# Gated linear attention, routed experts and a gated layer in one kernel: the last attention unit, the first pass's transposes and the last routing step change places

## The chip, the cores and the metric

The kernel runs on one core of a Trainium2 chip, as one launch. Time is device time in microseconds (us), and lower is better. The kernel before has a median of 864.84 us over three runs (859.22, 864.84 and 869.75 us). A core has five engines that run side by side and meet at semaphores: PE (matrix products; its weight loads are shown apart as PEld), DVE (vector), ACT (activation), POOL (general purpose, and here the issuer of indirect DMAs) and SP (issuer of the other DMAs). Each runs its own instructions strictly in the order written.

## The reference: what is computed

Three stages follow one another. `q`, `k`, `v` and `f_logit` are [4, 8, 768, 48]; there are 3072 tokens of 384 numbers.

```python
f = 1.0 / (1.0 + np.exp(-f_logit))
for t in range(S):                                   # attention: a decayed running state per head
    state = f[:, :, t, :, None] * state + np.einsum('bhd,bhe->bhde', k[:, :, t], v[:, :, t])
    y[:, :, t] = np.einsum('bhd,bhde->bhe', q[:, :, t], state)
...
logits = x @ w_gate                                  # experts: each token goes to one of 8
e_idx = np.argmax(logits, axis=1)
gate_w = probs[np.arange(N), e_idx]                  # probs: softmax of the logits
eom = 1.0 / (1.0 + np.exp(-(x @ w_output_gate)))
for e in range(E):
    h = np.maximum(x[mask] @ w1[e], 0.0)
    out[mask] = gate_w[mask, None] * eom[mask, e, None] * (h @ w2[e])
...
gate = 1.0 / (1.0 + np.exp(-(x @ w_gate)))           # gated layer, 384 -> 1536 -> 384
out = (gate * (x @ w_val)) @ w_out
```

## The kernel before, in words

**Attention** is cut into 24 units of 128 tokens (four sequences of six units). A loop `for i in range(1, NU)` writes the order by hand. In round i the kernel scores unit i (`s_score`, tile `pS`), makes keys `kT` and queries `qT` of unit i+1, masks the scores (`s_mask`, tile `am`), scans the logarithms of unit i+2 (`s_sum`, tile `ls`), forms the output of unit i-1 (`s_y`: products into `pY`, which ACT copies to `xT`), advances the state (`s_state`, tiles `pM`, `sn`), transposes the keys of the next unit (`s_turn`, tile `pk`), transposes `xT` back to rows (`s_rows`, tile `px`, copied by ACT to `x`) and takes 16 logits from `xT` (`s_logit`, tile `plg`, copied by DVE to `lg`).

**Routing** runs over groups of units: 0 to 5, 6 to 11, 12 to 16, 17 to 21 and 22 to 23. `route(u0, n)` is a generator of three parts: the arg max on DVE (`m` to `oh`), the selected gate (`ohf`, `sel`), and then the rank of each token in its expert (small products into `pr` on PE, then some thirteen short DVE operations up to the factor `meta` and the count `carry`). `pr`, `plg` and the throw-away products of `keep_warm` share one bank of PSUM, so each waits until DVE has read the one ahead of it. `put_rows` then scatters the rows of routed units to HBM by indirect DMAs from POOL, after a small POOL copy that writes factor and number behind each row.

**Experts** run as nine passes. The first (p = 0) takes the first 192 rows of expert 0, which the routing of units 0 to 16 has filled. Its rows are gathered at the start of round 23, scaled by their factors on DVE (`scale`), transposed on PE (`to_xt`, tile `ptx`), and cast by ACT and DVE to a high and a low part (`xt`). A pass has 8 steps f; each makes 9 products into `ph` (`proj`), then `hh` on ACT and `hl` on DVE, and two steps later 9 products into `po` (`down`). The second pass takes the rest of expert 0 (304 rows), the others the experts 1 to 7 in the order of a plan that is made on the chip from the counts (`make_plan`, with one product into `pf` that sums the counts). The loads of the next expert's weights and the gather of the third pass's rows go by the plan, since the expert's number stands in their addresses; the gather of the second pass's rows waits for the last scatter alone. After the passes comes the gated layer, six groups of 512 tokens.

**The stretch that the change touches** lies between round 17 and the start of the second pass. Before, the order there is: rounds up to 23, `scale`, `s_y(23)`, `to_xt(0)`, two DMAs of token numbers (`put_ids`), the rest of the routing of units 17 to 21, five scatters; then the first pass, with `s_rows(23)` and `s_logit(23)` behind its step 0, the first part of the last routing behind step 1, and the rest of it, two scatters, the gather of the second pass and the plan behind step 2. The output `xT` of unit 23 and the rows of units 19 to 23 lie in slots of the weight ring, which outlive the attention's memory; the other rows lie in a pool of the attention stage.

Of the kernel before, what the change touches and what calls it, by code (L numbers as in the profile page):

```python
# [8 lines left out]
F32 = mybir.dt.float32  # L9
# [11 lines left out]
P = 128  # L21
# [7 lines left out]
def kernel(  # L29
# [17 lines left out]
    nc = tc.nc  # L47
# [6 lines left out]
    HP = H // 2  # L54
# [3 lines left out]
    NU = B * NCH  # L58
# [11 lines left out]

    SOON = 12

    LATE = 19

    W0 = 192

# [2 lines left out]
    PD = P // 2 + D  # L79
# [3 lines left out]


    NWARM = 22
    WARM = (2, 2, 3)

    const = ctx.enter_context(tc.tile_pool(name="const", bufs=1))
    drp = ctx.enter_context(tc.tile_pool(name="drp", bufs=1, space=DRAM))
# [138 lines left out]
    def kill(key):  # L228
        dead.setdefault(key, len(dead))

    ring_s = Slots(ring, "ring", NRING)
# [141 lines left out]
    puts = []  # L373

    def put_rows(most):
        for u in puts[0:most]:
            nc.gpsimd.tensor_copy(xrow[u][:, DM:XW].bitcast(I32), meta[:, u, :].bitcast(I32))
            put = nc.gpsimd.indirect_dma_start(
                out=xs_all[:, :],
                out_offset=bass.IndirectOffsetOnAxis(ap=sidx[:, u : u + 1], axis=0),  # L380
                in_=xrow[u],
                in_offset=None,
                bounds_check=NSL - 1,
                oob_is_err=False,
            )

            tc.declare_no_dep(put.ins, group="rows", reason="distinct rows")
            tc.add_to_no_dep_group("rows", put.ins)
            del xrow[u]
            if u >= LATE:  # L390
                kill(("x", u))
            if u >= EARLY:
                tc.add_to_no_dep_group("late rows", put.ins)
            else:
                early_puts.append(put.ins)
        del puts[0:most]

    xts = {}
    xg = {}
# [93 lines left out]
    def s_logit(u):  # L493
        d = st.pop(u)
        pl = bank_po(MISC, [P, 2 * NE], "plg")
        for hp in range(HP):
            nc.tensor.matmul(pl, lhsT=d["xT"][:, hp, :], rhs=wgp[:, hp, :], start=(hp == 0), stop=(hp == HP - 1))  # L497
        nc.vector.tensor_copy(lg[:, u % (NU // 2), :], pl)
        if u >= LAST:
            kill(("xT", u))  # L500

    with ExitStack() as actx:
        ap1 = actx.enter_context(tc.tile_pool(name="ap1", bufs=1))
# [125 lines left out]
        def s_y(u):  # L629

            c = u % NCH
            d = st[u]
            pY = bank_po(1 + u % 2, [P, HP, P], "pY")
            so = sbd.get(u)
            vt = tin["v", u].rearrange("p h d -> p (h d)")

            for hp in range(HP):
                for j in range(2):
                    at = half(j, True)
                    h0 = (2 * hp + j) * D  # L640
                    nc.tensor.matmul(  # L641
                        pY[at, hp, :], lhsT=vt[:, h0 : h0 + at.stop - at.start], rhs=d["am"][:, j, hp, :],
                        start=(hp == 0), stop=(c == 0), skip_group_check=True,
                    )
            if c:
                for hp in range(HP):
                    for j in range(2):
                        at = half(j)
                        nc.tensor.matmul(  # L649
                            pY[at, hp, :], lhsT=so[at, hp, :], rhs=d["qT"][at, hp, :], start=False, stop=True,  # L650
                            skip_group_check=True,
                        )
            if u < LAST:
                xT = wk.tile([PD, HP, P], F32, name="xT")
            else:
                xT = ring_s.tile(("xT", u), [P, HP * P], F32, "xTlate").rearrange("p (h t) -> p h t", h=HP)[0:PD]
            nc.scalar.copy(xT, pY[0:PD])
            d["xT"] = xT

        with tc.manual_schedule():  # L660
# [52 lines left out]
            def step_route():  # L713
                if routing and next(routing[0], True):
                    routing.pop(0)

            def on(fn, u, *a):
                if 0 <= u < NU:
                    fn(u, *a)

            for i in range(1, NU):
                if i == NU - 1:
                    gather_rows(0)
                s_score(i)
                if i == 1:
                    s_log(i + 2)
                    s_mask(i, 0)
                on(s_keys, i + 1)
                on(s_queries, i + 1)
                load("qk", i + 4)  # L730
                on(s_end, i)
                put_rows(2 if i < 19 else 3 if i < 22 else 6)
                if i > 1:
                    on(s_log, i + 2)
                    s_mask(i, 0)
                load("f", i + 6)
                s_mask(i, 1)
                on(s_sum, i + 2)
                step_route()
                s_y(i - 1)  # L740
                load("v", i + 4)
                s_state(i)
                on(s_turn, i + 1)
                s_rows(i - 1)
                s_logit(i - 1)
                for u0, n in groups:
                    if i - 1 == u0 + n - 1:
                        routing.append(route(u0, n))
                if i > 16:
                    step_route()  # L750
                if i == 1:
                    nc.gpsimd.memset(zrow, 0.0)
                if 2 <= i < 6:

                    for e in (2 * i - 4, 2 * i - 3):
                        nc.sync.dma_start(
                            xs_all[e * SLOT + LEAST : (e + 1) * SLOT, :].rearrange("(b p) d -> p b d", p=P),
                            zrow[:, :, 0:XW].to_broadcast([P, NB - LEAST // P, XW]),
                        )
                if i == 6:  # L760
                    feed.issue()
                if i >= 8:
                    feed.step(1)
            while feed.left():
                feed.step()
            scale(xg[0], passes[0][2], nc.vector)
            s_y(NU - 1)
            to_xt(0, xg[0], passes[0][2])
            for part in range(2):
                put_ids(0, part)  # L770
            for todo in routing:
                for _ in todo:
                    pass
            put_rows(6)

    with ExitStack() as mctx:
        NGW, NGO = 17, 11
# [236 lines left out]
        with tc.manual_schedule():  # L1014
# [24 lines left out]
            for i in range(len(units) + LAG):  # L1039
# [13 lines left out]
                    )  # L1053
                    hs[i] = (hh, hl)
                if i == 0:
                    s_rows(NU - 1)
                    s_logit(NU - 1)
                if i == 1:
                    routing = route(*groups[-1])
                    next(routing)  # L1060
                if i - LAG in hs:
                    down(i - LAG)
                if i < len(units):
                    p, f = units[i]
                    if planning:
                        for _ in range(2):
                            next(planning, None)
                    elif i == 2:
                        for _ in routing:
                            pass  # L1070
                        put_rows(6)
                        gather_rows(1)
                        planning = make_plan()
                        next(planning)
                    if f == PUT_AT and p:
                        put_pass(p - 1)
                    if f == 0 and p:
                        turn(p + 1)
                    if p > 1 or p and f >= 2:
                        feed.step(3, ring_s.free)  # L1080
                    if p >= 2:
                        conv.step(1)
                    elif p:
                        conv.issue()
                    if len(who) == NE and not feed.left():
                        split_glu(1)
                    if i == 20:
                        check()
                    if f == 2 and ids_left is not None:
                        put_ids(ids_left, 1)  # L1090
                        ids_left = None
                    if f == (7 if p == 0 else 3 if p == 1 else 1) and p + 1 < len(passes):
                        scale(xg[p + 1], passes[p + 1][2], None if p else nc.vector)
                    if p == 0 and f == 7:

                        down(i - 1)
                        down(i)
                        keep_warm(WARM[2])
                    if f == (4 if p else 7) and p + 1 < len(passes):
                        to_xt(p + 1, xg[p + 1], passes[p + 1][2])  # L1100
                        put_ids(p + 1, 0)
                        ids_left = p + 1
                        if p:
                            gather_rows(p + 2)
                    if p == len(passes) - 1:
                        if f == 1:
                            gather_tok(0)
                        if f == 5:
                            tok_parts(0)
# [265 lines left out]
```

## Time and profile before

| | |
|---|---|
| median of three runs | 864.84 us (859.22 to 869.75) |
| the profiled execution | 866.66 us, span in the trace 865.0 us |
| PE busy | 843.2 us, 97% of the span |
| DVE, ACT, POOL busy | 463.4, 351.5, 211.2 us |
| granted PE clock, mean | 0.983 of full |
| attention, first pass, end of the last expert pass (us of the span) | 0 to 142, 142 to 172, to 403 |

The span runs from the first to the last instruction. In the rows below, a timeline row says: start, duration, engine, line, operation, output<-inputs, shapes and how many instructions were merged; in brackets the idle time of the engine ahead of it, and what ended that. Products are pipelined, so the step from one start to the next is what a product costs, not its duration. The granted clock is 1.00 at 2.4 GHz and 0.50 at 1.2 GHz.

### The profile page before, as it was taken

The numbers are of one execution on the slowest core, as the hardware profiler recorded it, in microseconds if no ns is written. First come the engines' busy times: TensorE is split into PE (matmuls) and PEld (weight loads), VectorE is DVE, ScalarE is ACT, GpSimd is POOL, SyncE is SP. The second block draws the span as 40 slices with busy tenths as digits, with TensorE's granted clock in tenths as the row PEclk, the third lists the DMA queues.
The fourth block names the chain that finished last, engine by engine and source line by source line (L and its number), as shares of the span: only waits on it lengthen the run. The fifth ranks groups of instructions, "written<-read, shape, count | busy, mean of one in ns | idle before, by whom it ended". The sixth has DMA issues, their size and how long they took to land.

```text
span 865.0 us, 14074 instructions
## 1 busy us (share of the span) xinstructions
PE 843.2 (97%) x5388; PEld 750.7 (87%) x5388; DVE 463.4 (54%) x866; ACT 351.5 (41%) x690; POOL 211.2 (24%) x201
## 2 busy tenths in 40 slices
PE   8999988999999999999999999999999999999995
PEld 5898878998899999998888888888888888888884
DVE  6888994468899998996543223221322322132221
ACT  7778772166556655654333212211221221122111
POOL 4227482104344554553200100100010010001001
PEclk9999998799999999999999999999999999999998
DMA  8999641656567677733100200010020000001001
GB/s 186 281 277 274 177 138 62 212 162 193 186 198 228 204 220 219 235 98 118 36 1 1 74 1 0 19 56 1 1 74 0 1 19 20 1 0 37 1 1 40
DMA packets 51582, 87.57 MB, mean 101 GB/s; under 512 B 12810, under 2 KB 32690, under 8 KB 51506
## 3 DMA queue, kind: packets, MB, share of 16 engines
q1 hardware_dynamic: 44882, 62.97, 25.1%
q0 software_dynamic: 6624, 23.62, 8.5%
q8 instruction: 44, 0.72, 0.3%
q14 instruction: 32, 0.26, 0.1%
HBM read 68.35 MB, written 18.22 MB: 100 GB/s over the span
## 4 chain that ended last, share of the span: by engine, by line
issue 50%; PE 37%; DVE 4%; POOL 3%; DMA 3%; ACT 2%; SPq 0%; POOLq 0%; DVEq 0%; ACTq 0%
PE ph L787 4%; PE ph L788 4%; PE ph L789 4%; PE po L788 4%; PE po L787 4%; PE po L789 4%; POOL out_dram L1000 2%; PE pS L588 2%; PE pY L641 2%; PE plg L497 2%; PE pY L649 2%; DMA st<-in_moe_w_dram 2%; DMA ft<-in_ft_dram 1%; PE ptx L423 1%; PE px L486 1%
## 5 line engine op out<-in xcount | busy, mean ns | idle before, releaser
L1131 DVE TENSOR_TENSOR hf<-pv,sg 128x512 f32<-128x512 f32 x72 | 49.8, 692 | 267.9 <-PE pv L789 264.1
L1000 POOL DMA_INDIRECT out_dram<-ob,ids x24 | 23.5, 980 | 404.2 <-DVE ob L999 398.7
L1127 ACT ACTIVATE sg<-pg 128x512 f32<-128x512 f32 x72 | 43.0, 598 | 173.9 <-PE pg L789 173.8
L1134 ACT CAST hh<-hf 128x512 fp32r<-128x512 f32 x72 | 44.7, 621 | 158.8 <-DVE hf L1131 158.8
L238 DVE TENSOR_TENSOR w_lo<-st,w_hi 128x384 fp32r<-128x384 f32 (+1 forms) x112 | 94.6, 875 | 9.5 <-ACT w_hi L237 8.5
L788 PE MATMUL po<-w_lo,hh 128*128 128x384 f32 x288 | 96.6, 335 | 0.0
L787 PE MATMUL po<-w_hi,hh 128*128 128x384 f32 x288 | 96.4, 335 | 0.0
L789 PE MATMUL po<-w_hi,hl 128*128 128x384 f32 x288 | 96.3, 334 | 0.0
L789 PE MATMUL pg<-xt_hi,w_lo 128*128 128x512 f32 x216 | 85.5, 396 | 0.0
L788 PE MATMUL pv<-xt_lo,w_hi 128*128 128x512 f32 x216 | 85.5, 396 | 0.0
L787 PE MATMUL pg<-xt_hi,w_hi 128*128 128x512 f32 x216 | 85.5, 396 | 0.0
L787 PE MATMUL pv<-xt_hi,w_hi 128*128 128x512 f32 x216 | 85.1, 394 | 0.0
L788 PE MATMUL pg<-xt_lo,w_hi 128*128 128x512 f32 x216 | 85.1, 394 | 0.0
L789 PE MATMUL pv<-xt_hi,w_lo 128*128 128x512 f32 x216 | 85.1, 394 | 0.0
L788 PE MATMUL po<-hl,w_hi 128*128 128x192 f32 (+8 forms) x216 | 75.7, 350 | 2.1 <-DVE hl L1051 2.1
L1135 DVE TENSOR_TENSOR hl<-hf,hh 128x512 fp32r<-128x512 f32 x72 | 49.9, 693 | 49.4 <-ACT hh L1134 49.4
L787 PE MATMUL po<-hh,w_hi 128*128 128x192 f32 (+8 forms) x216 | 75.7, 350 | 0.0
L789 PE MATMUL po<-hh,w_lo 128*128 128x192 f32 (+8 forms) x216 | 75.5, 350 | 0.0
L187 POOL TENSOR_SCALAR cva<-cva 128x512 f32<-128x512 f32 (+1 forms) x30 | 60.9, 2029 | 47.1 <-ACT cva L186 47.1
L1050 ACT ACTIVATE hh<-ph 128x192 fp32r<-128x192 f32 (+8 forms) x72 | 35.6, 494 | 85.9 <-PE ph L789 85.9
L787 PE MATMUL ph<-xt_hi,w_hi 128*128 128x304 f32 (+7 forms) x192 | 68.0, 354 | 0.9 <-DVE hl L1051 0.5
L237 ACT CAST w_hi<-st 128x384 fp32r<-128x384 f32 (+1 forms) x112 | 59.2, 558 | 20.1 <-PE po L788 20.0
(179 smaller groups left out, 1729.7 us busy)
## 6 DMA issues: line engine op xcount, KB each, us to landing
st<-in_moe_w_dram SPq DMA_DIRECT2D x48, 256.0 KB, 3.2
st<-in_moe_w_dram SPq DMA_DIRECT2D x32, 384.0 KB, 3.7
qk<-in_qkt_dram SPq DMA_DIRECT2D x48, 192.0 KB, 5.5
ft<-in_ft_dram SPq DMA_DIRECT2D x48, 96.0 KB, 5.5
v<-in_v_dram SPq DMA_DIRECT2D x24, 192.0 KB, 4.8
stg<-in_moe_w_gate_dram POOLq DMA_DIRECT2D x9, 512.0 KB, 4.0
stg<-in_moe_w_val_dram POOLq DMA_DIRECT2D x9, 512.0 KB, 3.9
stg<-in_moe_w_out_dram POOLq DMA_DIRECT2D x12, 384.0 KB, 3.4
```

The lines of the kernel that those rows point to most:

```text
L187: nc.gpsimd.tensor_scalar(out=af, in0=af, scalar1=HW_LEAST, scalar2=HW_MOST, op0=ALU.max, op1=ALU.min)
L237: nc.scalar.copy(hi, src)
L238: nc.vector.tensor_tensor(out=lo, in0=src, in1=hi.bitcast(F32), op=ALU.subtract)
L787: nc.tensor.matmul(ps, lhsT=ah, rhs=bh, start=first, stop=False)
L788: nc.tensor.matmul(ps, lhsT=ah, rhs=bl, start=False, stop=False)
L789: nc.tensor.matmul(ps, lhsT=al, rhs=bh, start=False, stop=last)
L1000: put = nc.gpsimd.indirect_dma_start(out=out[:, :], out_offset=bass.IndirectOffsetOnAxis(ap=idx[g][:, i : i + 1], axis=0), in_=ob, in_offs ...
L1050: nc.scalar.activation(out=hh, in_=pS, func=AF.Relu)
L1127: nc.scalar.activation(out=sg, in_=pg, func=AF.Sigmoid)
L1131: nc.vector.tensor_tensor(out=hf, in0=pv, in1=sg, op=ALU.mult)
L1134: nc.scalar.copy(hh, hf)
L1135: nc.vector.tensor_tensor(out=hl, in0=hf, in1=hh.bitcast(F32), op=ALU.subtract)
```

## The change

The last unit's output is computed in round 23, straight behind that of unit 22, and its `xT` lies in the attention's memory like the others. `scale` of the first pass's rows comes ahead of it. `to_xt(0)` follows the loop directly, then the rest of the routing of units 17 to 21 and its five scatters, and then `s_rows(23)`, `s_logit(23)`, the token numbers and the first part of the last routing. Its second part is issued behind step 0 of the first pass, its rest, the scatters, the gather and the plan behind step 1. In rounds 17 to 22 the extra routing step stands ahead of `s_rows` and of the line that appends a new group, so that a new group's first part runs one round later, behind that round's masks and scan. `put_rows` issues its copies first and then its scatters. Unit 18's rows move to the ring (`LATE`). At the end of the first pass one of three throw-away products goes, and the last `down` stands behind the transposes of the second pass.

```diff
-    LATE = 19
+    LATE = 18
...
-    WARM = (2, 2, 3)
+    WARM = (2, 2, 2)
...
         for u in puts[0:most]:
             nc.gpsimd.tensor_copy(xrow[u][:, DM:XW].bitcast(I32), meta[:, u, :].bitcast(I32))
+        for u in puts[0:most]:
             put = nc.gpsimd.indirect_dma_start(
...
-            if u < LAST:
-                xT = wk.tile([PD, HP, P], F32, name="xT")
-            else:
-                xT = ring_s.tile(("xT", u), [P, HP * P], F32, "xTlate").rearrange("p (h t) -> p h t", h=HP)[0:PD]
+            xT = wk.tile([PD, HP, P], F32, name="xT")
...
                 on(s_turn, i + 1)
+                if i == LAST:
+                    scale(xg[0], passes[0][2], nc.vector)
+                    s_y(i)
+                if i > 16:
+                    step_route()
                 s_rows(i - 1)
                 s_logit(i - 1)
                 for u0, n in groups:
                     if i - 1 == u0 + n - 1:
                         routing.append(route(u0, n))
-                if i > 16:
-                    step_route()
...
-            scale(xg[0], passes[0][2], nc.vector)
-            s_y(NU - 1)
             to_xt(0, xg[0], passes[0][2])
-            for part in range(2):
-                put_ids(0, part)
             for todo in routing:
                 for _ in todo:
                     pass
             put_rows(6)
+            s_rows(LAST)
+            s_logit(LAST)
+            for part in range(2):
+                put_ids(0, part)
+            routing = route(*groups[-1])
+            next(routing)
...
                 if i == 0:
-                    s_rows(NU - 1)
-                    s_logit(NU - 1)
-                if i == 1:
-                    routing = route(*groups[-1])
                     next(routing)
...
-                    elif i == 2:
+                    elif i == 1:
                         for _ in routing:
                             pass
                         put_rows(6)
...
                         down(i - 1)
-                        down(i)
                         keep_warm(WARM[2])
                     if f == (4 if p else 7) and p + 1 < len(passes):
                         to_xt(p + 1, xg[p + 1], passes[p + 1][2])
+                        if not p:
+                            down(i)
```

The rows below are the engines' instructions in the order written; the line numbers behind the change are one or a few off those of before.

First place: DVE in rounds 17 and 18, before. `lg` is the copy of unit 16's logits, with which the group 12 to 16 is complete.

```order
L498 COPY lg<-plg 128x16
L161 TENSOR_REDUCE m<-lg 128x5
L162 TENSOR_TENSOR t_1800<-lg,m 128x40
L163 TENSOR_TENSOR sc<-lg,m 128x40
L164 TENSOR_TENSOR sc<-sc,e_75 128x40
L165 TENSOR_REDUCE ms_all<-sc 128x5
L166 TENSOR_TENSOR oh<-sc,ms_all 128x40
L238 TENSOR_TENSOR w_lo<-st_1150,w_hi 128x512
L555 TENSOR_TENSOR kT<-qk_115,gi 112x512
L595 TENSOR_TENSOR am<-pS,tri 128x512 x2
L544 SCALAR_TENSOR_TENSOR ls<-runs_109,ln 112x512
```

The same place in the changed kernel:

```order
L499 COPY lg<-plg 128x16
L238 TENSOR_TENSOR w_lo<-st_1150,w_hi 128x512
L554 TENSOR_TENSOR kT<-qk_115,gi 112x512
L594 TENSOR_TENSOR am<-pS,tri 128x512 x2
L543 SCALAR_TENSOR_TENSOR ls<-runs_109,ln 112x512
L161 TENSOR_REDUCE m<-lg 128x5
L162 TENSOR_TENSOR t_1840<-lg,m 128x40
L163 TENSOR_TENSOR sc<-lg,m 128x40
```

The arg max of the group now stands behind the keys, the masks and the scan of the round, where it stood ahead of them.

Second place: PE behind the output of unit 23, before, and then behind the first products of the first pass, before.

```order
L641 MATMUL pY<-am,v 48x128
L649 MATMUL pY<-qT,sn 48x128 x8
L423 MATMUL ptx<-ident,xs 128x128 x3
L423 MATMUL ptx<-ident,xs 128x64 x3
L787 MATMUL ph<-xt_2381,w_hi 128x192
L788 MATMUL ph<-xt_2381,w_hi 128x192
```

```order
L788 MATMUL ph<-xt_2381,w_hi 128x192
L789 MATMUL ph<-xt_2381,w_lo 128x192
L486 MATMUL px<-ident,xTlate 128x112 x4
L497 MATMUL plg<-wgp,xTlate 128x16 x4
L787 MATMUL ph<-xt_2381,w_hi 128x192
```

The same two places in the changed kernel:

```order
L640 MATMUL pY<-am,v 48x128
L648 MATMUL pY<-qT,sn 48x128 x8
L487 MATMUL px<-ident,xT 128x112 x4
L498 MATMUL plg<-wgp,xT 128x16 x4
L424 MATMUL ptx<-ident,xs 128x128 x3
L424 MATMUL ptx<-ident,xs 128x64 x3
L330 LDWEIGHTS tris
L330 MATMUL pr<-oh,tris 128x40
```

```order
L336 LDWEIGHTS oneb
L336 MATMUL pr<-carry,oneb 128x40
L487 MATMUL px<-ident,xT 128x112 x4
L788 MATMUL ph<-xt_2354,w_hi 128x192
L789 MATMUL ph<-xt_2354,w_hi 128x192
L790 MATMUL ph<-xt_2354,w_lo 128x192
L498 MATMUL plg<-wgp,xT 128x16 x4
L788 MATMUL ph<-xt_2354,w_hi 128x192
```

The rows and logits of unit 22 now stand behind the output of unit 23; the routing products and unit 23's rows stand between the transposes `ptx` and the first `ph`, and unit 23's logits behind the first three of nine `ph`.

Third place: PE around the plan's product `pf`, before, and in the changed kernel.

```order
L788 MATMUL po<-hl,w_hi 128x192
L789 MATMUL po<-hh,w_lo 128x192
L884 MATMUL pf<-chk,onec 1x10
L787 MATMUL ph<-xt_2381,w_hi 128x192
L788 MATMUL ph<-xt_2381,w_hi 128x192
```

```order
L789 MATMUL po<-hl,w_hi 128x192
L790 MATMUL po<-hh,w_lo 128x192
L885 MATMUL pf<-chk,onec 1x10
L788 MATMUL ph<-xt_2354,w_hi 128x192
L789 MATMUL ph<-xt_2354,w_hi 128x192
```

Before, `pf` stands behind 36 `ph` and 18 `po` of the first pass; now behind 27 `ph` and 9 `po`.

## Rows read from the trace of the kernel before

**Rows 1.** The page: busy time, share and instructions of PE.

```profile
PE   843.2 (97%) x5388; PEld 750.7 (87%) x5388; DVE 463.4 (54%) x866; ACT 351.5 (41%) x690; POOL 211.2 (24%) x201
```

**Rows 2.** Busy time by stretch: length, engines' busy time, granted clock, DMA.

```profile
140.00:142.00 2.00, 1.08 (x12) 0.63 (x8) 1.33 (x7) 0.59 (x1) 0.78 (x2) 1.00 0.00 0
142.00:143.00 1.00, 0.68 (x4) 0.42 (x3) 0.65 (x3) 0.76 (x3) 0.72 (x3) 0.89 0.17 31
143.00:145.00 2.00, 2.00 (x11) 2.00 (x12) 0.24 (x1) 0.10 (x1) 1.72 (x3) 0.50 0.51 188
163.00:164.00 1.00, 1.00 (x9) 1.00 (x9) 0.34 (x1) 0.33 (x1) 0.00 (x0) 0.87 0.98 353
173.00:395.00 222.00, 221.48 (x1210) 209.44 (x1211) 195.92 (x317) 130.20 (x264) 102.78 (x81) 1.00 0.62 191
```

**Rows 3.** Timeline of PE, end of attention to the first pass.

```profile
136.30 0.60 PE L486 MATMUL px<-ident,xT 112*128 112x112 f32 x4 [0.69 <-ACT xT L657]
...
137.98 0.18 PE L330 MATMUL pr<-oh,tris 128*128 128x40 bf16 x1 [0.26 <-DVE lg L498]
...
139.24 1.08 PE L649 MATMUL pY<-qT,sn 48*48 48x128 f32 x16
141.24 0.85 PE L423 MATMUL ptx<-ident,xs 128*128 128x128 f32 x6 [0.92 <-PE pY L649]
142.37 0.35 PE L787 MATMUL ph<-xt,w_hi 128*128 128x192 f32 x1 [0.28 <-ACT xt L404]
```

**Rows 4.** Timeline of PE in the first pass.

```profile
143.94 0.41 PE L787 MATMUL ph<-xt,w_hi 128*128 128x192 f32 x1
144.16 0.41 PE L788 MATMUL ph<-xt,w_hi 128*128 128x192 f32 x1
...
152.78 0.24 PE L330 MATMUL pr<-oh,tris 128*128 128x16 bf16 x1
...
156.98 0.20 PE L884 MATMUL pf<-chk,onec 128*1 128x10 f32 x2
...
165.70 0.27 PE L789 MATMUL po<-hh,w_lo 128*128 128x192 f32 x1
165.81 0.27 PE L787 MATMUL po<-hh,w_hi 128*128 128x192 f32 x1
```

**Rows 5.** Timeline of PE, rounds 18 and 19.

```profile
110.01 0.18 PE L330 MATMUL pr<-oh,tris 128*128 128x40 bf16 x1 [1.19 <-DVE lg L498]
...
114.59 0.60 PE L576 MATMUL pk<-ident,kT 112*128 112x112 f32 x4 [1.72 <-DVE kT L555]
```

**Rows 6.** Timeline of DVE, rounds 16 and 19: the same short operation twice.

```profile
97.22 0.17 DVE L175 SCALAR_TENSOR_TENSOR ss<-eg,ss 128x6 f32<-128x6 f32 x1
...
111.68 1.21 DVE L175 SCALAR_TENSOR_TENSOR ss<-eg,ss 128x5 f32<-128x5 f32 x1
```

**Rows 7.** Timeline of POOL, round 19.

```profile
111.59 1.27 POOL L564 TENSOR_TENSOR qT<-qk,ls 112x512 f32<-112x512 f32 x1 [1.07 <-ACT gc_all L569]
```

**Rows 8.** Timeline of PE, end of the first pass.

```profile
170.17 0.82 PE L305 MATMUL pw<-oneb 128*128 128x512 bf16 x3
170.83 1.13 PE L423 MATMUL ptx<-ident,xs 128*128 128x128 f32 x9
172.34 0.41 PE L787 MATMUL ph<-xt_hi,w_hi 128*128 128x304 f32 x1 [0.38 <-ACT xt_hi L404]
```

**Rows 9.** Timeline of POOL: the last scatter.

```profile
157.45 0.97 POOL L378 DMA_INDIRECT xs_all<-xlate,sidx  x1 [0.28 <-POOL xlate L377]
```

**Rows 10.** Timeline of SP's queue: gathers for the second and third pass.

```profile
160.51 2.57 SPq L452 DMA_DIRECT2D xs<-xs_all  x3
```

**Rows 11.** Timeline of DVE: last routing and plan's sums, then the second pass's scale.

```profile
153.10 0.17 DVE L341 TENSOR_TENSOR t<-pr,oh 128x16 f32<-128x16 f32 x1 [1.01 <-PE pr L336]
...
155.79 0.25 DVE L881 TENSOR_REDUCE chk<-okl 112x1 f32<-112x96 f32 x1
...
167.99 1.06 DVE L434 TENSOR_SCALAR xs<-xs 128x384 f32<-128x384 f32 x3
```

More of the change, by code (lines that the diff above doesn't have):

```diff
@@ L498, in s_logit @@
         nc.vector.tensor_copy(lg[:, u % (NU // 2), :], pl)
-        if u >= LAST:
-            kill(("xT", u))
     with ExitStack() as actx:
```

## The prediction, made before the changed kernel was run

> **What bounds the kernel now.** I read the page first: PE is busy for 843.2 of 865.0 us [rows 1], so time is lost where PE waits or where its clock is low, and little elsewhere. Next the table of stretches, to see where that is. From the second pass to the end of the last expert pass PE works 221.48 of 222.00 us at a granted clock of 1.00 [rows 2]. It has no slack there: whatever the stretch ahead of it gains or loses reaches the end unchanged. Ahead of it, two things show. Around 142 us PE is busy for only 1.08 of 2.00 us, and the granted clock then drops to 0.50 and comes back between 163 and 164 us [rows 2]. A mean of 0.89 between 142 and 143 puts the fall at 142.78 (1 for 0.78 us, 0.5 for the rest), and 0.87 puts the rise at 163.26, so the low stretch is 20.5 us. Then the timeline of PE, for the waits by name: at the end of attention [rows 3], in the first pass [rows 4], in rounds 18 and 19 [rows 5], and at the start of the second pass [rows 8]. Last DVE, POOL and SP, to see what those waits wait for and what covers the work that is moved [rows 6, 7, 9 to 11].
>
> The sum goes against the profiled execution, 866.66 us, which is 1.82 us above the median of the three runs. These lie 10.5 us apart, so a change of less than about 1% (8.6 us) can't be told from none.
>
> **Term 1, the routing step of rounds 17 to 22.** Before, the arg max of a group stands on DVE ahead of the keys `kT`, and PE waits 1.72 us for `kT`; the rank products `pr` stand right behind the logits on PE and wait 1.19 us until DVE has read the shared bank [rows 5], together 2.91 us. In the new order the keys, masks and scan come first and `pr` stands ahead of rows and logits, so neither reason is left. Next late is `xT`, the ACT copy that `s_rows` needs: `pr` used to come behind it and now PE reaches it sooner. A wait for such a copy took 0.69 us [rows 3]; I leave that, so 2.91 - 0.69 = **-2.2 us**, between -2.9 (it is covered) and 0 (DVE, with its work unchanged in number, is merely late elsewhere).
>
> One price here may move: a short operation of a routing step took 1.21 us in place of 0.17 [rows 6] while POOL formed `qT` for 1.27 us [rows 7]. The group's third part now runs a round later and at another place of the round; the delay of 1.04 us may go or recur, and lies within the bounds. The Trainium skill, "SBUF — State Buffer", section "Who interferes with whom", says that DVE and GpSimd share a port pair under an exclusive lock; the two rows agree with that, and it speaks against any order that puts DVE's two-input operations beside POOL's, as the moved arg max may be: by it the term would be 1.04 us smaller if the delay meets the masks that PE waits for.
>
> **Term 2, the head of the first pass.** Before, PE waits 0.69 for `xT`(22), 0.26 for the logits' bank, 0.92 ahead of `ptx` (the row names `pY`, long done; what ends then is the `scale` on DVE, which stands behind the routing) and 0.28 for the cast `xt` [rows 3], 2.15 us in all. In the change `pY`(23), 1.08 us and its first half [rows 3], covers `xT`(22); `scale` stands ahead of the ranks; and the ranks' products and `px`(23) lie between `ptx` and the first `ph` and cover the casts. Added is a wait: `plg`(23), three products into the first `ph`, needs the bank that DVE empties with the first rank operation, now behind the three casts `xt_lo`. Three products at 0.11 [rows 4] cover 0.33 of the casts' length; by the nearest waits for that bank, 0.26 [rows 3] and 1.19 [rows 5], it costs 0.26 to 1.19, and as the casts begin under `px`(23) I take 0.5. So 0.5 - 2.15 = **-1.65 us**, between -1.0 and -2.15.
>
> **Term 3, the low clock.** At half clock one product of the first pass takes 0.22 us from start to start, at full clock 0.11 [rows 4]; over many of them 0.213 and 0.111. So 20.5 us hold 96 products and cost 96 x 0.102 = 9.8 us, 0.48 per us. The fall comes behind a stretch in which PE was interrupted again and again, though by no wait over 0.92 us [rows 3], and the rise 6.3 us after `pf` at 156.98 [rows 4], the last time that the pass's dense products are interrupted. In the change `pf` stands behind 36 instead of 54 of them: 18 x 0.213 = 3.8 us earlier relative to the first `ph`, and `px`(23), some 0.9 us at half clock (0.60 at full [rows 3]), goes ahead of that `ph`. From the first `ph` to `pf` it was 14.6 us and becomes 9.9; with the same 6.3 behind it and the fall again 0.4 behind the first `ph`, the low stretch is 15.8 us. 4.7 x 0.48 = **-2.3 us**. The bounds are the rivals below: no low stretch, the same one, or a longer one.
>
> **Term 4, the end of the first pass.** There PE waits 0.38 us for the high part of the second pass's rows [rows 8]. The last `down`, nine products or 1.0 us, now stands there and covers it. One throw-away product goes too: three start 0.66 us before the next instruction [rows 8], 0.22 each. They filled time in which PE had to wait for the rows, and so did `down`; I count 0.38 + 0.22 and up to 0.3 of waits of the first `ph` that the casts follow: **-0.9 us**, between 0 (PE only reaches `ptx` sooner and waits for the scaled rows) and -0.9.
>
> **At nothing.** The gather of the second pass needs the last scatter, which ends at 158.4 [rows 9], and goes out at 160.5 [rows 10]; its `scale` at 168.0 follows without idle time of DVE [rows 11]. All of it starts some 7 to 8 us earlier (a step of the pass, 18 products at 0.213, and 3.9 us of terms 1 and 2), the transposes only about 7, so the distance stays; gone, each us of a late gather would cost one at `ptx`. POOL's copies ahead of its scatters delay the first scatter by the later copies and not the last. SP's sequence is the same, so no transfer is moved past another. The slots of the ring change by one tile.
>
> Sum: -2.2 - 1.65 - 2.3 - 0.9 = -7.05, that is 859.6 us on the profiled execution and, 1.82 lower, 857.8 for the median.
>
> **Rivals.** *A, the clock does not fall.* For it: two of the waits ahead of `ph` go, and none of the four was long. The 9.8 us come back whole. Against this, at full clock DVE is too slow for the new places: `pr`(23) stands 15 products (1.7 us) behind `plg`(23), while lg, eight routing operations and `hl` take some 2.9 us at the rows' 0.17 to 0.25 each, so PE waits 1.2; and between `pr` and `pf` stand 18 products (2.0 us), against 2.9 us of ranks and checks [rows 11] and an `hl`, so it waits 1.4. Terms 1, 2 and 4 with this: -4.75 - 9.8 + 2.6 = -11.95, 854.7, or 852.9 for the median. Beside it stands the Trainium skill, "TensorE: Matmul & The Clock Gate", section "Loop structure matters more than you think": products back to back keep the clock, long waits lose it. By it the head of the pass should keep its clock in both kernels; the trace agrees only in part, since the clock fell with no wait above 0.92 us. *B, the gain is hidden.* PE gets to the first pass sooner, but the low stretch stays 20.5 us, since it ends when it ends, and half of terms 1 and 4 turns into waits for `xT` and the scaled rows: -1.1 - 1.65 - 0.45 = -3.2, 863.5, median 861.6. For it: the waits of [rows 5] are DVE's, which is no less loaded. *C, slower: a longer low stretch.* `px`(22), `plg`(22), `ptx`, `pr`, `px`(23) and then `plg`(23), `pr` and `pf` within 36 products are more interruptions in a row than before, three of them with a DVE answer ahead. If the clock falls already at `ptx` and the interruptions hold it until the second pass begins, it is low for some 33 us: (33 - 20.5) x 0.48 = +6.0, and `ptx`, `pr` and `px` at half speed add 1.0. With terms 1, 2 and 4 that makes +2.25, 868.9, median 867.1. It decides from a low stretch of 28 us on, where the loss is 4.75 with that 1.0. Against it: before, with the same three kinds of interruption, the clock rose 6.3 us after the last of them.
>
> **How the numbers follow.** The forecast has 0.52, A 0.25, B 0.15, C 0.08. The likeliest gives 858 us. The range runs from A, 852.9, to B with nothing left of terms 1 and 4, 861.6 + 1.55 = 863.2, and 2 us further on either side, since profiled run and median differ by as much (1.82 here): 851 to 865. C is left out, and about a tenth of the others. Over 1% faster is below 856.2: nearly all of A and a fifth of the forecast, together 0.35. Over 1% slower, above 873.5, needs C with a low stretch that goes on into the second pass: 0.03. Within 1%: 0.62.
>
> **What would show it.** Term 1: the waits at `pr` and `pk` in rounds 18 to 20 are gone, and together under 0.8 us remain ahead of `px`. Term 2: the first `ph` starts near 138.6 us (142.37 - 2.2 - 2.15 + 0.6 for `px`(23)), with work and not waits ahead of it, and a wait of about half a us at `plg`(23). Term 3: `pf` some 10 us behind the first `ph`, the granted clock at 0.50 for about 16 us. Term 4: no wait at the second pass's first `ph`, which starts near 165 us (160 in A), and no new one at `ptx`. The prediction is wrong if the low stretch is not 13 to 18 us, or if PE waits for the scaled rows.

## The result, and the profile after

The changed kernel has a median of 855.15 us over 14 runs (853.20 to 857.49), beside 864.56 us for the kernel before; the ratio is 0.9905, with a 95% interval of 0.9883 to 0.9928. Seven later runs gave 856.03 us and 0.9921 (0.9892 to 0.9950). The kernel is faster by 0.8 to 1%, some 7 to 9 us. The execution profiled first is the slowest of the 14: 857.49 us, with a span of 855.8 us. Two runs of the kernel before, of 871.0 us each, count as a slower state and are left out below; with them its mean low clock would be 23.2 us in place of 22.9.

The page's first line: PE works 4.3 us less than in [rows 1], in a span that is 9.2 us shorter.

```profile
PE 838.9 (98%) x5387; PEld 746.6 (87%) x5387; DVE 462.7 (54%) x866; ACT 350.7 (41%) x690; POOL 210.9 (25%) x201
```

The table of stretches, columns as in [rows 2].

```profile
17.00:18.00 1.00, 1.00 (x11) 0.97 (x13) 1.00 (x2) 0.28 (x2) 0.33 (x1) 0.85 1.01 313
...
21.00:22.00 1.00, 1.00 (x18) 0.80 (x16) 1.00 (x3) 0.00 (x0) 1.00 (x1) 0.95 0.99 201
...
132.00:139.00 7.00, 7.00 (x102) 5.93 (x98) 3.60 (x14) 2.20 (x7) 0.00 (x0) 1.00 0.07 16
139.00:140.00 1.00, 0.94 (x7) 0.57 (x6) 0.97 (x5) 0.76 (x4) 0.00 (x0) 1.00 0.00 0
140.00:141.00 1.00, 1.00 (x9) 1.00 (x9) 0.86 (x7) 0.00 (x0) 0.00 (x0) 0.79 0.00 0
...
141.00:154.00 13.00, 13.00 (x64) 12.74 (x65) 8.84 (x54) 1.52 (x6) 9.01 (x16) 0.50 0.36 117
...
154.00:155.00 1.00, 1.00 (x10) 1.00 (x10) 0.05 (x1) 0.33 (x1) 0.00 (x0) 0.89 0.87 270
```

Read as in the prediction, the clock is low from 140.58 to 154.22 us, 13.6 us in place of 20.5. A short low stretch of 3.4 us, from 17.7 us on, lies ahead of all that the change touches, and one of 3.4 us near 399 us, which the profiled execution of before had, is missing here. So single executions differ in stretches that the change doesn't reach.

Timeline of PE, the rows that answer to [rows 3, 4, 5, 8].

```profile
113.90 1.06 PE L498 MATMUL plg<-wgp,xT 112*128 112x16 f32 x8 [0.25 <-DVE t L341]
...
118.91 0.60 PE L575 MATMUL pk<-ident,kT 112*128 112x112 f32 x4 [0.23 <-DVE kT L554]
...
136.44 0.60 PE L487 MATMUL px<-ident,xT 112*128 112x112 f32 x4
...
137.71 0.85 PE L424 MATMUL ptx<-ident,xs 128*128 128x128 f32 x6
138.50 0.19 PE L330 MATMUL pr<-oh,tris 128*128 128x40 bf16 x1
...
139.24 0.36 PE L788 MATMUL ph<-xt,w_hi 128*128 128x192 f32 x1
...
139.54 0.27 PE L790 MATMUL ph<-xt,w_lo 128*128 128x192 f32 x1
139.88 1.28 PE L498 MATMUL plg<-wgp,xT 112*128 112x16 f32 x8
...
148.50 0.20 PE L885 MATMUL pf<-chk,onec 128*1 128x10 f32 x2
...
162.42 0.60 PE L305 MATMUL pw<-oneb 128*128 128x512 bf16 x2
162.87 1.13 PE L424 MATMUL ptx<-ident,xs 128*128 128x128 f32 x9
163.93 0.36 PE L788 MATMUL po<-hh,w_hi 128*128 128x192 f32 x1
...
165.01 0.32 PE L788 MATMUL ph<-xt_hi,w_hi 128*128 128x304 f32 x1
```

Of the brackets that [rows 3, 5, 8] show, none is left; two new ones, of 0.25 and 0.23 us, stand in rounds 19 and 20. `ptx`, `ph` and the second pass's `ph` follow the work ahead of them.

### The profile page after: what moved, and what is told of

It reads as the page before. It is cut to its first block, busy times and chain, and to the rows that moved or that the text cites. A ratio compares the mean times of both kernels' runs of the same rounds, so it can differ in the third digit from the quotient of the medians.

```text
span 855.8 us, 14071 instructions
## 1 busy us (share of the span) xinstructions
PE 838.9 (98%) x5387; PEld 746.6 (87%) x5387; DVE 462.7 (54%) x866; ACT 350.7 (41%) x690; POOL 210.9 (25%) x201
## 4 chain that ended last, share of the span: by engine, by line
issue 50%; PE 39%; POOL 3%; DVE 3%; ACT 3%; DMA 1%; POOLq 0%; SPq 0%; DVEq 0%; ACTq 0%
PE ph L788 5%; PE po L789 4%; PE po L788 4%; PE po L790 4%; PE ph L789 4%; PE ph L790 4%; PE pS L587 2%; PE pY L640 2%; POOL out_dram L1001 2%; PE pY L648 2%; PE plg L498 2%; DMA ft<-in_ft_dram 1%; PE ptx L424 1%; PE px L487 1%; POOL cva L187 1%
```

## The experiments

**How they are read.** The time of a run goes with its low clock, the us that PE spends at half clock, which I work out as 2 x (1 - mean granted clock) x span; about 5 us of it lie behind PE's last product and cost nothing, in every kernel. All 226 runs whose clock is on record, with one level for each kernel and one price for low clock, give 0.371 us (0.348 to 0.395) for each us of it and a scatter of 1.08 us. The level is the time at equal low clock: it holds waits and work, while the clock stands apart, as far as one price serves for all kernels. Each ± is a 95% interval. The runs were on several chips; at the same low clock the kernel before stands 0.5 to 0.6 us higher on one than on the other of the two that measured it most. On the higher one were e1, e2, e3 and e5, so their levels may be too high by as much.

| kernel | median us | ratio to before (95%) | mean low clock, us | level against the changed kernel, us |
|---|---|---|---|---|
| before (101 runs) | 863.64 | | 22.9 | +4.35 ± 0.54 |
| changed (21 runs) | 855.65 | 0.9905, 0.9921 | 14.3 | 0 |
| e1_step_back (12) | 859.92 | 0.9950 (0.9917 to 0.9982) | 23.2 | +1.01 ± 0.79 |
| e6_only_step (12) | 856.81 | 0.9932 (0.9912 to 0.9953) | 11.3 | +2.17 ± 0.77 |
| e10_fill (12) | 859.35 | 0.9977 (0.9950 to 1.0004) | 19.5 | +2.53 ± 0.77 |
| e12_last_back (5) | 857.00 | 0.9896 (0.9878 to 0.9915) | 16.1 | -0.47 ± 1.05 |
| e5_head_back (11) | 856.03 | 0.9916 (0.9889 to 0.9943) | 11.8 | +1.67 ± 0.79 |
| e3_end_back (11) | 857.58 | 0.9939 (0.9913 to 0.9965) | 15.6 | +1.51 ± 0.79 |
| e2_rest_late (12) | 856.60 | 0.9922 (0.9897 to 0.9948) | 15.7 | +0.46 ± 0.76 |
| e9_more_pf (12) | 858.61 | 0.9945 (0.9910 to 0.9980) | 21.2 | +0.55 ± 0.78 |
| e8_warm_head (9) | 855.33 | 0.9916 (0.9887 to 0.9944) | 10.8 | +1.29 ± 0.84 |
| e11_sums_early (8) | 855.87 | 0.9919 (0.9889 to 0.9949) | 13.0 | +1.07 ± 0.88 |

**The two kernels again.** 

> The kernel before, unchanged, for the granted clock of each of its runs. Theory (the low stretch differs from run to run): mean clocks spread as the times do, 0.97 to 0.99, and a run with a lower clock is a slower one, by about 0.48 us for each us of low clock. Rival (the 10 us of spread come from elsewhere, such as transfers): the same clock in all runs.

 

> The changed kernel, unchanged, for the granted clock of more of its runs and as the measure of the two kernels beside it. Expected: ratio 0.990, low clock of a run 5 to 20 us, median about 12.

 Measured: before 863.60 us, ratio 1.0022 (0.9991 to 1.0053), mean clocks from 0.977 (870.79 us) to 0.991 (859.23 us); the changed kernel 856.03 us, mean clocks 0.987 to 0.993, median low clock 15.4 us. The lottery of the clock is in both kernels, and the change shifts it. The profiled execution of before that was taken here had 3.4 us of low clock in the first pass, where the one of [rows 2] had 20.5.

**The routing step, undone and alone.**

```diff
+                if i > 16:
+                    step_route()
                 s_rows(i - 1)
                 s_logit(i - 1)
...
-                if i > 16:
-                    step_route()
```

e6 puts this into the kernel before and changes nothing else; e1 takes it out of the changed kernel. 

> The changed kernel with the routing step of rounds 17 to 22 back behind rows and logits. Theory (each term of the sum stands by itself): the waits of 1.2 us at pr and 1.7 us at pk in rounds 18 and 19 come back, the round of unit 20 begins some 2.4 us later, and the time is 2.4 us above the changed kernel's 855.2: 857.6. Rival (the gain is the clock's, PE has slack in the attention): the waits come back, the time stays within 0.6 us of 855.2.

 

> The kernel before with only the routing step of rounds 17 to 22 moved. Theory: the round of unit 20 begins 2.4 us earlier and the time is 2.4 us less, 862.2. Rival (PE has slack, or the later routing delays the first pass): within 0.6 us of the kernel before, 864.6.

 Measured: e6 gains 6.5 us by itself between the means, of which 2.18 ± 0.70 is level and the rest low clock (22.9 to 11.3 us). e1 loses 4.3 us against the changed kernel: 1.0 is level, the rest low clock (14.3 to 23.2). Both theory and rival fell short: in e6 the waits are worth what the sum said, and the low clock, 11.6 x 0.371 = 4.3 us, is worth twice that. The four kernels agree: without the moved step the mean low clock is 22.9 us (before) and 23.2 (e1), with it 11.3 (e6) and 14.3 (changed). e1's PE shows the wait at `pr` back, and a low clock from 109.1 us on (`pS` of 16 products takes 2.08 us where it takes 1.16 at full clock):

```profile
109.56 0.19 PE L330 MATMUL pr<-oh,tris 128*128 128x40 bf16 x1 [1.19 <-DVE sel L171]
...
109.82 2.08 PE L587 MATMUL pS<-qT,kT 48*128 48x128 f32 x16
...
116.93 1.16 PE L587 MATMUL pS<-qT,kT 48*128 48x128 f32 x16
...
139.99 0.18 PE L330 MATMUL pr<-oh,tris 128*128 128x40 bf16 x1 [0.27 <-DVE lg L499]
...
143.16 0.49 PE L789 MATMUL ph<-xt,w_hi 128*128 128x192 f32 x1 [0.63 <-DVE xt L406]
```

The wait at `pk`, 1.72 us in [rows 5], is missing in this execution: PE at half clock is slow enough for DVE. It is missing too in the later execution of the kernel before, whose clock was low from 111.25 to 114.66 us. So low clock costs less in these rounds, which may be why e1's level lies only 1.0 us above; that is argued and not shown.

e10 puts throw-away products into the two waits of e1.

```diff
+                if i == 19:
+                    fill(7)
                 on(s_turn, i + 1)
...
+                if i == 18:
+                    fill(5)
                 if i > 16:
                     step_route()
```

> The changed kernel with the routing step of rounds 17 to 22 back (as in e1_step_back), and with throw-away products in the two waits that come back with it: five ahead of pr in round 18, seven ahead of pk in round 19, so that PE works there instead of waiting. Theory (a wait costs its own length and lets the clock fall as well): the waits' 2.4 us stay, the low clock goes back from a median of 25.7 us a run to the changed kernel's 12, time about 2.4 us above the changed kernel, ratio 0.993. Rival (the moved step lowers the clock's loss in another way, for example by when DVE reaches the first pass): low clock stays near 24 us, ratio 0.995 or above.

 Measured: level +2.53, as the theory said for the waits; low clock 19.5 us on average, 5.1 ± 2.7 more than the changed kernel and 3.7 ± 4.0 less than e1, which chance alone can give. In its profiled execution the clock holds from 104 to 142 us:

```profile
104.00:142.00 38.00, 36.80 (x503) 30.93 (x502) 30.82 (x73) 22.60 (x51) 22.98 (x25) 1.00 0.38 113
144.00:145.00 1.00, 0.41 (x2) 0.42 (x3) 0.97 (x6) 0.00 (x0) 0.77 (x6) 0.55 0.00 0
```

It is low from 144.1 us on, while a `ph` waits 0.63 us. So it isn't shown that low clock follows the waits of rounds 18 and 19, and single executions speak against it: with both waits the clock stayed up in the execution of [rows 2], whose first fall came at 142.78 us, and without them it was low for 3.4 us from 115.1 us on in e3 and from 115.5 in e6. e12 undoes the step in rounds 22 and 23 alone, which brings the wait at `ph` back.

```diff
-                if i > 16:
+                if 16 < i < 22:
                     step_route()
...
+                if i >= 22:
+                    step_route()
```

> The changed kernel with the routing step back behind rows and logits in rounds 22 and 23 alone; rounds 17 to 21 stay changed. Undoing all rounds gave low clock of a median of 25.7 us a run and 4.5 to 4.7 us more time; filling its waits of rounds 18 and 19 left 18.9 us. Theory (the rest of that low clock comes from the head of the first pass, where pr again waits 0.26 us for its bank and a ph 0.63 us for the casts behind the ranks): low clock about 19 us a run, time 2 to 3 us above the changed kernel, ratio 0.993 to 0.995. Rival (it comes from rounds 18 and 19 and from when the pass begins): low clock 12 to 15 us as in the changed kernel, time at most 0.9 us more, ratio 0.991 to 0.992.

 Measured: the theory's low clock (18.8 us in four of five runs), but a ratio below even the rival's; on this chip the kernel before had 30.4 us in seven runs, 7.5 above its mean. This settles nothing. The fifth run had no low clock at work at all and took 850.97 us: what that kernel costs at full clock. Its PE then waits for DVE in the pass:

```profile
138.94 0.36 PE L791 MATMUL ph<-xt,w_hi 128*128 128x192 f32 x1 [0.63 <-DVE xt L406]
...
144.74 0.20 PE L887 MATMUL pf<-chk,onec 128*1 128x10 f32 x2 [1.49 <-DVE chk L884]
```

**The head and the end of the first pass.** e5 puts `scale` and the output of unit 23 back behind the loop; e3 undoes the end of the pass.

```diff
-                if i == LAST:
-                    scale(xg[0], passes[0][2], nc.vector)
-                    s_y(i)
...
+            scale(xg[0], passes[0][2], nc.vector)
+            s_y(LAST)
             to_xt(0, xg[0], passes[0][2])
```

```diff
-    WARM = (2, 2, 2)
+    WARM = (2, 2, 3)
...
                         down(i - 1)
+                        down(i)
                         keep_warm(WARM[2])
...
-                        if not p:
-                            down(i)
```

> The changed kernel with scale and the output of unit 23 back behind the loop, all else as changed. Theory: PE waits about 0.7 us for xT of unit 22 and 0.9 us for xT of unit 23 or the scaled rows, time +1.6: 856.8. Rival (the clock decides, these waits only move its fall): low stretch one step of some 3.4 us longer or shorter and the time 855.2 with 1.6 either way, whatever the waits are.

 

> The changed kernel with the end of the first pass as before: three throw-away products and the last down ahead of the transposes. Theory: 0.38 us of wait ahead of the second pass's first ph and one product of 0.22 come back, time +0.6 to +0.9: 855.8 to 856.1. Rival (PE waits there for the scaled rows anyway): 855.2, with the wait at ptx in place of the one at ph.

 Measured: levels of +1.67 and +1.51. Of the two waits named for e5 the one for `xT` is there, 0.69 us, and the one of 0.9 us is not; from the last `pS` to the first `ph` PE takes 8.80 us where the changed kernel takes 7.94, so the trace accounts for 0.86 of the 1.67. The rival's 855.2 ± 1.6 holds the time as well, since e5 had less low clock; only the level speaks for the theory. In e3 the wait is the one named, 0.38 us for `xt_hi`, and none stands at `ptx`, so the rival is out; the level is above the 0.6 to 0.9 asked for, but its interval reaches down to 0.72. PE of e5, then of e3:

```profile
136.34 0.60 PE L487 MATMUL px<-ident,xT 112*128 112x112 f32 x4 [0.69 <-ACT xT L653]
...
145.53 0.17 PE L330 MATMUL pr<-oh,tris 128*128 128x16 bf16 x1 [0.83 <-DVE oh L166]
```

```profile
162.19 0.82 PE L305 MATMUL pw<-oneb 128*128 128x512 bf16 x3
162.85 1.14 PE L424 MATMUL ptx<-ident,xs 128*128 128x128 f32 x9
164.36 0.41 PE L788 MATMUL ph<-xt_hi,w_hi 128*128 128x304 f32 x1 [0.38 <-ACT xt_hi L405]
```

**What holds the clock down.** e2 moves the last route's rest, and with it the scatters, the gather and `pf`, one step back; e9 repeats `pf` at steps 3 and 4; e8 adds large products ahead of the ranks.

```diff
-                    elif i == 1:
+                    elif i == 2:
```

```diff
+            again.append(chk)
...
+                    if i in (3, 4):
+                        nc.tensor.matmul(bank_po(MISC, [1, NE + 2], "pf2"), lhsT=onec, rhs=again[0], start=True, stop=True)
```

```diff
+            keep_warm(4)
             for todo in routing:
```

> The changed kernel with the rest of the last routing, its scatters, the gather and the plan behind step 2 of the first pass, as before, and pf behind 54 of its products. Theory (the clock rises a set time after pf): the low stretch grows by 18 half-clock products, 3.8 us (13.4 to about 17 in the profiled execution), time +1.8: 857.0. Rival (the end of the low stretch doesn't follow pf): low stretch and time unchanged within 0.6, 855.2, or a little less, since DVE has longer for the ranks.

 

> The changed kernel with the plan's product pf done again, into a bank that nobody reads and with nothing to wait for, at steps 3 and 4 of the first pass. Theory (every such interruption holds the clock down): the rise comes one or two steps of 3.8 us later, low stretch 17 to 21 us, time +1.8 to +3.6: 857 to 858.8. Rival (pf holds the clock only through its wait, or not at all): the same low stretch, time +0.2: 855.4.

 

> The changed kernel with four throw-away products of 512 columns ahead of the ranks' products, between ptx and pr. Theory (the clock falls in this stretch whatever is added, and rises after pf): +0.9 us, 856.1. Rival (the fall comes from the many small products in a row, and a few large ones hold the clock): no low stretch in the first pass, 0.48 us saved for each of up to 13 us of it, less 0.9 and up to 2.6 of new waits for DVE: 852 to 854.

 Measured: e2 has 1.4 ± 2.7 us more low clock on average and its mean is 1.0 us higher, so the theory's 3.8 us and no change at all are both still possible. e9 has 6.9 ± 5.1 us more low clock and is 3 us slower, as the theory said; beside the changed kernel's seven runs on the same chip it is 4.1 ± 5.6, so the size is not known. Timeline of PE in e9, and its stretches:

```profile
145.53 0.20 PE L887 MATMUL pf<-chk,onec 128*1 128x10 f32 x2 [1.48 <-DVE chk L884]
...
149.31 0.20 PE L1066 MATMUL pf<-chk,onec 128*1 128x10 f32 x2
...
153.53 0.20 PE L1066 MATMUL pf<-chk,onec 128*1 128x10 f32 x2
```

```profile
146.00:147.00 1.00, 1.00 (x8) 1.00 (x7) 0.81 (x6) 0.00 (x0) 0.92 (x1) 0.59 0.53 198
147.00:159.00 12.00, 12.00 (x59) 11.56 (x59) 2.68 (x13) 0.99 (x3) 3.48 (x7) 0.50 0.74 248
159.00:160.00 1.00, 1.00 (x7) 1.00 (x7) 0.00 (x0) 0.22 (x1) 0.00 (x0) 0.59 0.94 259
```

The clock falls behind the wait of 1.48 us and rises at 159.82, 6.3 us after the last of the added products, none of which waited: the distance of [rows 4] again. But the record has executions in which that distance is no rule. In the second profiled execution of the changed kernel the clock rose at 148.16 us, and in e2's at 148.06, both ahead of `pf`; in e2's `pf` then waited 1.06 us and the clock stayed up. Stretches, and PE's `pf`, of the changed kernel and then of e2:

```profile
142.00:148.00 6.00, 6.00 (x32) 5.96 (x31) 4.66 (x32) 1.30 (x5) 4.60 (x9) 0.50 0.28 102
148.00:149.00 1.00, 1.00 (x10) 0.86 (x9) 0.55 (x4) 0.00 (x0) 0.73 (x1) 0.92 0.47 176
...
148.41 0.20 PE L885 MATMUL pf<-chk,onec 128*1 128x10 f32 x2
```

```profile
149.00:155.00 6.00, 4.93 (x45) 4.73 (x45) 5.11 (x32) 0.66 (x3) 3.66 (x7) 1.00 0.28 102
...
151.58 0.20 PE L885 MATMUL pf<-chk,onec 128*1 128x10 f32 x2 [1.06 <-DVE chk L882]
```

In e3, e5, e6, e8 and e12 too `pf` waited 1.21 to 1.63 us at full clock, and no low stretch of the pass followed. So what holds the clock down in the pass is not settled. e8 lowers the low clock by 3.5 ± 2.8 us, worth 1.3 us, and pays 1.29 us of level for its four products: the two cancel. Its profiled execution has no low stretch in the first pass, as its rival said, but those of e3, e5, e6 and e12, without its products, have none either.

**A shorter way to `pf`.** e11 sums the check of the decays in round 23 and puts the last group's count ahead of its factor.

```diff
-            nc.vector.tensor_copy(chk[:, 0:NE], carry[:, 0, :])
-            nc.vector.tensor_copy(chk[:, NE : NE + 1], early)
...
-        some(factor)
+        if u0 + n < NU:
+            some(factor)
...
+            nc.vector.tensor_tensor(out=chk[:, 0:NE], in0=carry[:, 0, :], in1=ct, op=ALU.add)
+            some(factor)
```

> The changed kernel with DVE's work ahead of the plan's product pf cut short: the check of the decays is summed in round 23, the last group's count goes into the check directly and ahead of its factor. Theory (in runs in which the clock holds, PE waits 1.2 to 1.6 us for DVE at pf): that wait falls under 0.4 us, time 0.5 to 1.2 us less than the changed kernel's, ratio 0.989. Rival (the time then goes to ptx, which waits for the gathered rows, since the last scatter starts no earlier): the wait at pf goes and one at ptx of the same length comes, ratio 0.9905.

 Measured: no gain, ratio 0.9919 beside 0.9921 for the changed kernel on the same chip. PE shows why the theory's half us to 1.2 us didn't come, though the wait at `pf` is gone, and the rival's place is wrong too:

```profile
143.20 0.17 PE L331 MATMUL pr<-oh,tris 128*128 128x16 bf16 x1 [0.84 <-DVE oh L167]
145.59 0.20 PE L887 MATMUL pf<-chk,onec 128*1 128x10 f32 x2
151.01 0.25 PE L799 MATMUL ph<-xt,w_hi 128*128 128x192 f32 x1 [1.03 <-issue]
151.75 0.35 PE L799 MATMUL ph<-xt,w_hi 128*128 128x192 f32 x1 [0.26 <-issue]
152.45 0.32 PE L800 MATMUL ph<-xt,w_hi 128*128 128x192 f32 x1 [0.35 <-issue]
```

1.64 us of waits for which the profile names no releaser follow at 150 to 152.5 us, and from 152.2 us on, in the last of them, the clock is low for 6.8 us. No kernel here is shown to beat the changed one.

## Why the prediction was right, and where it was not

858.0 us was forecast, 851 to 865; 855.15 was measured. By the levels and the low clock the gain of 7.54 us between the means (863.24 and 855.70) is 4.35 us of waits and work and (22.9 - 14.3) x 0.371 = 3.2 us of clock. The sum had 4.75 for terms 1, 2 and 4 and 2.3 for term 3. The size of both parts was near; the reason for the second was not, so that the total came out as near as it did is in part luck.

**Term 1 (forecast -2.2): right in size, and more than its own.** From the round of unit 18 to that of unit 23 PE took 29.31 us before and 27.21 after, 2.10 less. Start to start of `pS`, before, and then after:

```profile
103.12 1.16 PE L588 MATMUL pS<-qT,kT 48*128 48x128 f32 x16
...
132.43 1.16 PE L588 MATMUL pS<-qT,kT 48*128 48x128 f32 x16
```

```profile
104.09 1.16 PE L587 MATMUL pS<-qT,kT 48*128 48x128 f32 x16
...
131.30 1.16 PE L587 MATMUL pS<-qT,kT 48*128 48x128 f32 x16
```

e6 gives 2.18 and e10 2.53 by level, e1 only 1.0. The delay of [rows 6] beside POOL's `qT` recurred, on another operation: `sn` takes 1.73 us where it takes 0.36 a round later, while `qT` runs, and `kT` behind it makes PE wait the 0.23 us at `pk`. DVE, then POOL, after:

```profile
115.97 1.73 DVE L625 TENSOR_TENSOR sn<-sn,gc_all 112x192 f32<-112x192 f32 x1
...
121.46 0.36 DVE L625 TENSOR_TENSOR sn<-sn,gc_all 112x192 f32<-112x192 f32 x1
```

```profile
116.18 1.29 POOL L563 TENSOR_TENSOR qT<-qk,ls 112x512 f32<-112x512 f32 x1
```

The Trainium skill, "SBUF — State Buffer", section "Who interferes with whom", has DVE and GpSimd hold a shared port pair in turn; the two durations agree with that. The price at PE was the 0.23 us at `pk`, not 1.04.

**Term 2 (forecast -1.65): right, a little small.** From the last `pS` to the first `ph` it was 9.94 us and is 7.94, with `px`(23), 0.58 us, now in it: -2.58. The wait ahead of `plg`(23) is 0.23 us, not 0.5: behind the `ph` at 139.54 the next start was due 0.11 us later, at 139.65, and came at 139.88. Net -2.35. e5 prices the part that `scale` and the output hold at 0.86 us in the trace and 1.67 by level.

**Term 3 (forecast -2.3): the step that failed.** In the execution profiled first its numbers came out near: `pf` stands 9.26 us behind the first `ph` (9.9), the rise 5.72 us behind `pf` (6.3), the low stretch 13.6 us (15.8). But that was one draw. The forecast took the one 20.5 us stretch for the kernel's own; a second execution of before had 3.4 us in the first pass, and a second one of the changed kernel 6.8, which the prediction's own sign (13 to 18 us) counts against it; its variants had 13.6, 6.8 or none. The rule under the term, a rise some 6 us behind `pf`, failed in that second execution and in e2's, where the clock rose ahead of `pf`. The price was lower too: 0.371 for each us over all low stretches of the runs, in place of 0.48. What shifts the draws is not the place of `pf`: e6 leaves it where it was and has 11.3 us of low clock. The moved routing step shifts them, by 11.6 ± 2.1 us in e6 and 8.9 ± 4.0 the other way in e1. Why it does stays open: filling the waits of rounds 18 and 19 (e10) took back no more of e1's low clock than chance can give, and e12 doesn't settle whether the short waits at the head of the pass, or when the pass begins, make the rest.

**Term 4 (forecast -0.9): right in sign, larger.** In the profile: from `pw` to the second pass's `ph` 2.17 us before and 2.59 after with nine products (1.08) in it, -0.66; by level e3 says 1.51 ± 0.79. The profile's three terms add up to 5.1 us, where the level has 4.35 ± 0.54.

**At nothing.** In the execution profiled first `scale` of the second pass ends at 162.31 us, ahead of `ptx`, which doesn't wait; the second pass's first `ph` came at 165.01 us, where 165 was forecast. The cover held at full clock too: `ptx` doesn't wait in the profiled executions of e3, e5, e8 and e12. It waits for the scaled rows, 1.50 us in e6's and 0.56 in e2's, where the gather stands behind step 2, as before the change. **Rivals.** A, the clock that holds, is not one outcome but some of the executions: the changed kernel's run with the least low clock, 5.1 us, took 853.20 us, where A had 852.9. Its new waits came at about their price in variants at full clock: 0.83 us at `pr` in e3 and e5 (1.2 forecast), 1.2 to 1.6 at `pf` (1.4). B and C did not come.

## What to carry to other kernels

Where PE bounds a kernel, a wait that DVE causes in a dense stretch costs about its length; here the move that took such waits away also shifted the low clock, by about twice as much time in e6, for a reason that wasn't found. Look at the mean clock of many runs before taking one profile's low stretch, or its distance from some instruction, for a property of the kernel. With time against low clock on all runs, differences of 1 to 2 us show that medians with 10 us of spread hide. A gain that shows as less low clock should be tried part by part: here the part that seemed to carry it (the place of `pf`) did not.

## What the runs showed of the hardware

The clock fell at 140.58 us in the changed kernel although PE had worked 7.00 of 7.00 us and 0.94 of 1.00 us just ahead. What it had done there were small products: 16 columns (`plg`), 40 (`pr`), transposes of 64 to 128. The Trainium skill, "TensorE: Matmul & The Clock Gate", section "Loop structure matters more than you think", ties a warm engine to products that follow each other without long waits; here they did, and the clock fell all the same, so the measurement decides. In e11, whose PE has the same products in the same order there, the clock held until 152.2 us, so the products alone don't decide it either. The low stretches of the fourteen profiled executions, the end aside, lasted 3.4, 6.8, 13.6 or 20.5 us, and one execution had none. On the same input the changed kernel had between 5.1 and 22.3 us of low clock in a run, the kernel before between 12.0 and 40.0. And waits of PE without a releaser in the profile, 0.2 to 1.0 us each, stand some 4 to 7 us behind `pf` in the second profiled execution of the changed kernel and in those of e3, e5, e8 and e11, while the clock is up (1.03 us in e11); what they are wasn't found.
